# A GEGLU layer on one core: first phase over seven PSUM banks, four blocks of x transposed by TensorE

## The chip, the core and the metric

The kernel runs on one core of one Trainium2 chip. A core has five engines that run side by side and meet through semaphores: TensorE (PE; its weight loads are listed as PEld), VectorE (DVE), ScalarE (ACT), GpSimd (POOL) and SyncE (SP). Sixteen DMA engines move data between HBM and the on-chip memory SBUF. Matmul results go to PSUM, eight banks of 128 partitions by 512 fp32 values. The metric is the device time of one execution in microseconds (us), as the median of ten runs.

## The reference

```python
x: (32, 32, 1024) bf16    w_gate, w_up: (1024, 3584)    w_down: (3584, 1024)
def reference(x, w_gate, w_up, w_down):
    return (gelu_tanh(x @ w_gate) * (x @ w_up)) @ w_down
```

The leading dimensions of x make 1024 rows (tokens). 1024 is also the contraction length of the two first products: eight blocks of 128, called k here.

## The kernel before

**Tiling.** The tokens are two halves h of 512. The 3584 hidden columns are 28 chunks m of 128. One chunk and one half need a `g` product and a `u` product, each a PSUM bank that gathers eight matmuls, one for each k: 128 by 128 weights are loaded and 512 columns of x, transposed, stream past (`mm_gu`, L162). `glu` (L171) then lets ScalarE take the GELU of the `g` bank and VectorE multiply it by the `u` bank into `hT`. When all of `hT` is there, the second product runs, 28 matmuls for each of 17 output pieces, and each piece is copied and stored. Each matmul there needs the tokens' columns of `hT` as weights and `wd` as the moving operand.

**Order of work.** The program is a list that is written by hand: `pr.add` appends an operation to its engine's list with the keys that it reads and writes (`r`, `w`), and each engine runs its own list in order. Waits follow from the keys. A wait stops everything that stands behind it on the same engine, DMA issues included. The profile gives L98 for all operations, because they are all made by one line of `emit`.

**Start.** TensorE runs eight matmuls on constants (L184). x must get into `xT` with the contraction on the partitions. For half 0, blocks k=0 and 1 (`NX = 2`) are loaded plainly into `xn` by two transfers, one issued by SP and one by ACT (L191). TensorE transposes them in 128 by 128 pieces against an identity matrix, four for each block, and VectorE copies the bf16 result out of PSUM in halves of 256 columns (L205 to L212). The second half of a block has a key of its own, `("x", k, "b")`. All other blocks are transposed on the way by DMA, issued by SP (`load_x`, L195): k=2, 3, 4, 5 and 6-7 for half 0 at once, and four pairs for half 1 once a matmul of k=3 is done (L235).

Weights of the first four chunks come in pieces by k (`load_w`, L155): k=0 and 1 of `g` by SP and of `u` by ACT, 128 KB each; k=2-3 of each by ACT, 256 KB each; k=4-5 and k=6-7 of each by ACT once the last matmul of k=0, or of k=1, is done (L231). Weights of later chunks come from SP in 1 MB pieces behind that.

**First phase.** Half 0 of the chunks m=0 to 3 goes over all eight banks at once: for each k from 0 to 5, four `g` matmuls and four `u` matmuls (L221). Then, one m after another, the last two k of `g` and of `u`, and its `glu` (L223). Half 1 of the same chunks follows in a like order, starting with k=0 and 1 of each m.

Of the kernel before, what the change touches and what calls it, by code (L numbers as in the profile page):

```python
# [6 lines left out]
P = 128  # L7
BF16 = mybir.dt.bfloat16
FP32 = mybir.dt.float32
F32R = mybir.dt.float32r  # L10
ACTF = mybir.ActivationFunctionType
# [93 lines left out]
def bass_standalone__geglu_ffn__sampling_kernel(  # L105
# [11 lines left out]
    DK, TC, FM = D // P, N // P, F // P  # L117
# [3 lines left out]
    x_r = xf.rearrange("(tc p) d -> p tc d", p=P)  # L121
# [4 lines left out]
    pr = _Program()  # L126

    with ExitStack() as es:
        def sb(name, shape, dtype):
            return es.enter_context(nc.sbuf_tensor(name, shape, dtype))  # L130

        xT = sb("xT", [P, DK, N], BF16)
# [7 lines left out]
        g_b = [sb(f"g{i}", [P, 512], FP32) for i in range(NGB)]  # L140
        warm = sb("warm", [P, 2], FP32)
        ident = sb("ident", [P, P], BF16)
        xn = sb("xn", [P, 4, 2 * P], BF16)
        osb = xT
        ps = es.enter_context(nc.psum_tensor("ps", [P, 8, 512], FP32))
        const0 = nc.const_aps.tensor(0.0, [P, 1], FP32)
# [8 lines left out]
        def load_w(eng, kind, gi, k0=0, k1=DK, r=()):  # L155
            c0, n, buf, s0 = groups[gi]
            src, dst = (wg_r, wg_b) if kind == "g" else (wu_r, wu_b)
            pr.add(eng, "dma_start", dst[buf][:, k0:k1, s0 * P:(s0 + n) * P], src[:, k0:k1, c0 * P:(c0 + n) * P],
                w=[(kind, buf, s0 + i, k) for i in range(n) for k in range(k0, k1)],
                r=r, dma=f"w{kind}{gi}_{k0}")  # L160

        def mm_gu(kind, m, h, k, bank, w=()):  # L162
            buf, slot = where[m]
            wt = (wg_b if kind == "g" else wu_b)[buf]
            pr.add("pe", "matmul", ps[:, bank, :], wt[:, k, slot * P:(slot + 1) * P], xT[:, k, h * 512:(h + 1) * 512],
                start=(k == 0), stop=(k == DK - 1),
                r=[(kind, buf, slot, k), ("x", k, h)] + ([("x", k, "b")] if h == 0 else []), w=[("ps", bank), *w])

        glu_n = [0]

        def glu(m, h, bg, bu):  # L171
            g = glu_n[0] % NGB
            glu_n[0] += 1
            pr.add("act", "activation", g_b[g][:, :], ps[:, bg, :], ACTF.Gelu_apprx_tanh,
                   r=[("ps", bg)], w=[("gb", g)])
            pr.add("dve", "tensor_tensor", hT[:, m, h * 512:(h + 1) * 512], g_b[g][:, :], ps[:, bu, :], ALU.mult,
                r=[("gb", g), ("ps", bu)], w=[("h", m, h)])
# [8 lines left out]

        NX = 2
        for i, eng in enumerate(("sp", "act")):  # L190
            pr.add(eng, "dma_start", xn[:, 2 * i:2 * i + 2, :], x_r[:, 2 * i:2 * i + 2, 0:NX * P], w=[("xn", i)], dma=f"xn{i}")  # L191
        for k in range(NX):
            load_w("sp", "g", 0, k, k + 1)
            load_w("act", "u", 0, k, k + 1)
        def load_x(h, k0, k1, r=()):  # L195
            pr.add("sp", "dma_start_transpose", xT[:, k0:k1, h * 512:(h + 1) * 512],
                   xf[h * 512:(h + 1) * 512, k0 * P:k1 * P], r=r, w=[("x", k, h) for k in range(k0, k1)],
                   dma=f"x{k0}_{h}")

        for k0, k1 in ((2, 3), (3, 4), (4, 5), (5, 6), (6, 8)):  # L200
            load_x(0, k0, k1)
        load_w("act", "g", 0, 2, 4)
        load_w("act", "u", 0, 2, 4)
        pr.add("act", "activation", warm[:, 0:1], const0, ACTF.Gelu_apprx_tanh)
        for k in range(NX):  # L205
            for i, b in enumerate((6, 7) if k == 0 else (4, 5)):
                half = ps[:, b, 0:P].bitcast(BF16)
                for t in range(2):
                    pr.add("pe", "transpose", half[:, t * P:(t + 1) * P], xn[:, 2 * i + t, k * P:(k + 1) * P],
                           ident[:, :], r=[("xn", i), "ident"], w=[("ps", b)])  # L210
                pr.add("dve", "tensor_copy", xT[:, k, i * 256:(i + 1) * 256], half, r=[("ps", b)],
                       w=[("x", k, 0) if i == 0 else ("x", k, "b")])  # L212


        KO = 2
        for h in range(2):
            steps = []
            for m in range(4):
                steps += [(m, kind, k) for kind in "gu" for k in range(KO)] if h else []
            for k in range(KO if h else 0, DK - KO):  # L220
                steps += [(m, kind, k) for kind in "gu" for m in range(4)]  # L221
            for m in range(4):
                steps += [(m, kind, k) for kind in "gu" for k in range(DK - KO, DK)] + [(m, None, None)]  # L223
            for m, kind, k in steps:
                if kind is None:
                    glu(m, h, 2 * m, 2 * m + 1)
                else:
                    mm_gu(kind, m, h, k, 2 * m + (kind == "u"), w=[("mm", k)] if h == 0 and m == 3 and kind == "u" else ())
                if h == 0 and (m, kind) == (3, "u"):
                    if k < 2:  # L230
                        load_w("act", "g", 0, 2 * k + 4, 2 * k + 6, r=[("mm", k)])  # L231
                        load_w("act", "u", 0, 2 * k + 4, 2 * k + 6)
                    if k == 3:
                        for k0 in range(0, DK, 2):
                            load_x(1, k0, k0 + 2, r=[("mm", k)])  # L235
# [7 lines left out]
        u = 8  # L243
        for m in range(4, FM):
            for h in range(2):
                bg, bu = 2 * (u % 4), 2 * (u % 4) + 1
                for kind, b in (("g", bg), ("u", bu)):
                    for k in range(DK):
                        mm_gu(kind, m, h, k, b)
                glu(m, h, bg, bu)  # L250
                u += 1
            for gi in range(loaded + 1, len(groups)):
                if groups[gi][0] - 6 <= m:
                    load_w("sp", "g", gi)
                    load_w("sp", "u", gi)
                    loaded = gi
            if m >= 4 and m % 3 == 0 and wd_pieces:
                a, b_ = wd_pieces.pop(0)
                pr.add("sp", "dma_start", wd[:, a:b_, :], wd_r[:, a:b_, :],
                       r=[("h", m - 1, 1)], w=[("wd", i) for i in range(a, b_)], dma=f"wd{a}")  # L260
# [9 lines left out]
        for ji, (tc, col, n) in enumerate(jobs):  # L270
            b = ji % 8
            for m in range(FM):
                pr.add("pe", "matmul", ps[:, b, 0:n], hT[:, m, tc * P:(tc + 1) * P], wd[:, m, col:col + n],
                    start=(m == 0), stop=(m == FM - 1),
                    r=[("h", m, tc // 4), ("wd", m)], w=[("ps", b)])
            if ji % 2 == 0:
                pr.add("act", "activation", osb[:, tc, col:col + n], ps[:, b, 0:n], ACTF.Copy,
                       r=[("ps", b)], w=[("o", ji), ("x", tc, 0), ("x", tc, 1), ("x", tc, "b")])
            else:
                pr.add("dve", "tensor_copy", osb[:, tc, col:col + n], ps[:, b, 0:n],  # L280
                       r=[("ps", b)], w=[("o", ji), ("x", tc, 0), ("x", tc, 1), ("x", tc, "b")])
            pr.add("sp", "dma_start", out_r[:, tc, col:col + n], osb[:, tc, col:col + n],
                   r=[("o", ji)], dma="out")
# [34 lines left out]
```

## Time and profile before

| What | Value |
|---|---|
| Median of ten runs | 300.18 us (299.79 to 301.03) |
| The profiled execution | 300.05 us, its span 298.3 us |
| TensorE matmuls | busy 294.4 us (99%), x1388 |
| TensorE weight loads | busy 135.7 us (45%) |
| VectorE, ScalarE | busy 44.7 us (15%), 40.1 us (13%) |
| Matmuls 128x512 on wg and on wu | x448 each, mean 379 ns |
| Transposes by TensorE | x8, mean 304 ns |
| VectorE copies of 128x256 bf16 into xT | x4, mean 289 ns |
| DMA transposes | x9 issued by SP, median 5.8 us to landing |
| HBM | 22.28 MB read, 2.10 MB written |

The span is the time from the first to the last instruction that the profiler recorded; the rest of the execution's time lies around it. Busy time is summed over instructions as they are recorded, and a matmul's recorded length holds its way through the array, which overlaps with the next one. For TensorE, then, the distance from one start to the next tells the rate, and the length does not. In a timeline, rows that follow each other on one engine with the same form are merged: start, time from the first start to the last end, engine, line, operation, output and inputs, shapes and count; in brackets the idle time ahead of them and what ended it.

### The profile page before, as it was taken

Reading aid. Unit: us, or ns where it says so; the run is one execution under the profiler, and the core shown is the slowest. Engines: PE = TensorE matmul, PEld = TensorE weight load, DVE = VectorE, ACT = ScalarE, POOL = GpSimd, SP = SyncE. Lnnn points to the kernel's source line nnn. Section 1 sums busy time; section 2 is a strip of 40 time slices with the busy share of each in tenths; the row PEclk is TensorE's granted clock in tenths of the full one; section 3 lists DMA queues with packets and bytes.
Section 4 is the critical chain, followed back from the end, with each engine's and each line's share of the span. In section 5 each row is a group of like instructions: output and inputs, shape, how many; then the busy total and the mean of one; then the engine's idle time right before and its main releaser. Section 6 shows DMA issues by size and latency. Waiting matters only on the chain.

```text
span 298.3 us, 3155 instructions
## 1 busy us (share of the span) xinstructions
PE 294.4 (99%) x1388; PEld 135.7 (45%) x1388; DVE 44.7 (15%) x68; ACT 40.1 (13%) x67; POOL 0.7 (0%) x6
## 2 busy tenths in 40 slices
PE   8999999999999999999999999999999999999996
PEld 4344444444444444444444444444444444444455
DVE  1030421111221111221111122110000000000000
ACT  1030411211111121111121111110000000000000
POOL 0000000000000000000000000000000000000000
PEclk9999999999999999999999999999999999999999
DMA  7999744006608408331040030000000000010001
GB/s 163 264 244 355 230 152 119 24 0 209 215 0 288 138 11 284 128 80 62 0 143 0 0 141 2 0 0 18 20 18 34 20 18 18 18 37 18 18 18 37
DMA packets 28845, 26.42 MB, mean 89 GB/s; under 512 B 8224, under 2 KB 25248, under 8 KB 28832
## 3 DMA queue, kind: packets, MB, share of 16 engines
q1 hardware_dynamic: 26640, 24.25, 26.3%
q10 hardware_dynamic: 2192, 1.97, 2.7%
q8 instruction: 11, 0.18, 0.2%
q14 instruction: 2, 0.02, 0.0%
HBM read 22.28 MB, written 2.10 MB: 82 GB/s over the span
## 4 chain that ended last, share of the span: by engine, by line
PE 97%; DMA 2%; ACT 0%; issue 0%
PE ps L98 97%; DMA wg<-in_w_gate_dram 2%; ACT xT L98 0%
## 5 line engine op out<-in xcount | busy, mean ns | idle before, releaser
L98 PE MATMUL ps<-xT,wg 128*128 128x512 bf16 x448 | 108.1, 379 | 0.6 <-DMA wg<-in_w_gate_dram 0.5
L98 PE MATMUL ps<-xT,wu 128*128 128x512 bf16 x448 | 108.1, 379 | 0.0
L98 PE MATMUL ps<-wd,hT 128*128 128x512 bf16 (+1 forms) x476 | 96.9, 366 | 0.0
L98 PEld LDWEIGHTS ps<-wd,hT 128*128 128x128 bf16 x476 | 46.6, 98 | 50.4
L98 PEld LDWEIGHTS ps<-xT,wg 128*128 128x128 bf16 x448 | 43.6, 98 | 54.0 <-DMA wg<-in_w_gate_dram 1.5
L98 PEld LDWEIGHTS ps<-xT,wu 128*128 128x128 bf16 x448 | 43.8, 98 | 52.9 <-DMA wu<-in_w_up_dram 0.5
L98 DVE TENSOR_TENSOR hT<-g,ps 128x512 bf16<-128x512 f32 x56 | 38.5, 688 | 156.4 <-PE ps L98 156.4
L98 ACT ACTIVATE g<-ps 128x512 f32<-128x512 f32 x56 | 33.4, 597 | 159.5 <-PE ps L98 159.5
L98 DVE CAST xT<-ps 128x512 bf16<-128x512 f32 (+1 forms) x8 | 5.3, 658 | 88.1 <-PE ps L98 88.1
L98 ACT ACTIVATE xT<-ps 128x512 bf16<-128x512 f32 (+1 forms) x9 | 5.2, 573 | 93.1 <-PE ps L98 93.1
L98 PE MATMUL ps<-const-bfloat16-1.0 128*128 128x512 bf16 (+1 forms) x8 | 2.9, 545 | 0.8 <-PEq L303 0.8
L98 PEld LDWEIGHTS ps<-const-bfloat16-1.0 128*128 128x128 bf16 x8 | 1.0, 137 | 2.4 <-issue 2.4
L98 ACT ACT_TABLE_LOAD x1 | 1.3, 1283 | 3.5 <-issue 3.5
L98 DVE COPY xT<-ps 128x256 bf16<-128x256 bf16 x4 | 0.9, 289 | 4.0 <-PE ps L98 4.0
L98 PE MATMUL ps<-ident,xn 128*128 128x128 bf16 x8 | 1.0, 304 | 0.0
L98 PEld LDWEIGHTS ps<-ident,xn 128*128 128x128 bf16 x8 | 0.7, 132 | 0.2
L98 POOL TENSOR_SCALAR_AFFINE_SELECT ident<-ident 128x128 bf16<-128x128 bf16 x1 | 0.3, 292 | 0.2 <-POOL ident L98 0.2
L98 POOL MEMSET ident<- 128x128 bf16 x1 | 0.2, 204 | 0.3 <-POOLq L303 0.3
L98 ACT ACTIVATE warm<-const-float32-0.0 128x1 f32<-128x1 f32 x1 | 0.2, 203 | 0.0
L303 POOL MEMSET const-bfloat16-1.0<- 128x1 bf16 x1 | 0.1, 102 | 0.0
L303 POOL MEMSET const-uint8-127<- 128x1 uint8 x1 | 0.1, 102 | 0.0
L303 POOL MEMSET const-float32-0.0<- 128x1 f32 x1 | 0.1, 98 | 0.2 <-issue 0.2
(1 smaller groups left out, 0.1 us busy)
## 6 DMA issues: line engine op xcount, KB each, us to landing
wd<-in_w_down_dram SPq DMA_DIRECT2D x7, 1024.0 KB, 5.4
wg<-in_w_gate_dram SPq DMA_DIRECT2D x6, 1024.0 KB, 7.3
wu<-in_w_up_dram SPq DMA_DIRECT2D x6, 1024.0 KB, 9.6
out_dram<-xT SPq DMA_DIRECT2D x15, 128.0 KB, 1.7
wg<-in_w_gate_dram ACTq DMA_DIRECT2D x3, 256.0 KB, 6.3
wu<-in_w_up_dram ACTq DMA_DIRECT2D x3, 256.0 KB, 6.7
wg<-in_w_gate_dram SPq DMA_DIRECT2D x2, 128.0 KB, 3.5
wu<-in_w_up_dram ACTq DMA_DIRECT2D x2, 128.0 KB, 4.2
```

The source lines that it names most:

```text
L98: ins = getattr(eng, name)(*args, **kw)
L303: nc = _bacc.Bacc("TRN2", target_bir_lowering=False, num_devices=1)
```

## The change

The first phase of half 0 uses seven banks. Bank 7 is left to transposes, and `u` of m=3 is done in one go at the end of the half. TensorE transposes four blocks of x (`NX = 4`). Those of block 0 stand where they stood, in banks 6 and 7, with two copies of 256 columns. Those of k=1, 2 and 3 stand between the matmuls of the block before: after `g` of m=0 and 1, ahead of `g` of m=2 and 3 and `u` of m=0 to 2. They go to bank 7, and one copy of 512 columns takes each out. The columns of x for k=2 and 3 come by a plain transfer from SP, behind the first weights. The DMA transposes of half 0 shrink to k=4, 5 and 6-7, and the first of them waits for the second copy of block 0. The weights for k=2 and 3 come in four pieces of 128 KB instead of two of 256 KB, still by ACT. What was released by the last `u` matmul of m=3 (L229) is now released by that of m=2.

```diff
-                r=[(kind, buf, slot, k), ("x", k, h)] + ([("x", k, "b")] if h == 0 else []), w=[("ps", bank), *w])
+                r=[(kind, buf, slot, k), ("x", k, h)] + ([("x", k, "b")] if h == k == 0 else []), w=[("ps", bank), *w])
...
-        NX = 2
+        NX = 4
...
+        pr.add("sp", "dma_start", xn[:, :, 2 * P:NX * P], x_r[:, 0:4, 2 * P:NX * P],
+               w=[("xn", 0, 1), ("xn", 1, 1)], dma="xn2")
+        for k in range(2, 4):
+            load_w("act", "g", 0, k, k + 1)
+            load_w("act", "u", 0, k, k + 1)
...
-        for k0, k1 in ((2, 3), (3, 4), (4, 5), (5, 6), (6, 8)):
-            load_x(0, k0, k1)
-        load_w("act", "g", 0, 2, 4)
-        load_w("act", "u", 0, 2, 4)
...
+        def pe_x(k):
+            for i in range(2):
+                b = 6 + i if k == 0 else 7
+                half = ps[:, b, (0 if k == 0 else i * P):(P if k == 0 else (i + 1) * P)].bitcast(BF16)
                 for t in range(2):
                     pr.add("pe", "transpose", half[:, t * P:(t + 1) * P], xn[:, 2 * i + t, k * P:(k + 1) * P],
-                           ident[:, :], r=[("xn", i), "ident"], w=[("ps", b)])
+                           ident[:, :], r=[("xn", i, k // 2), "ident"], w=[("ps", b)])
...
+            if k:
+                pr.add("dve", "tensor_copy", xT[:, k, 0:512], ps[:, 7, 0:256].bitcast(BF16), r=[("ps", 7)],
+                       w=[("x", k, 0)])
+
+        pe_x(0)
+        for k0, k1 in ((4, 5), (5, 6), (6, 8)):
+            load_x(0, k0, k1, r=[("x", 0, "b")])
...
+            if h == 0:
+                for k in range(DK - KO):
+                    steps += [(m, "g", k) for m in range(2)] + ([("x", None, k + 1)] if k + 1 < NX else [])
+                    steps += [(m, "g", k) for m in range(2, 4)] + [(m, "u", k) for m in range(3)]
...
+                for kind in "gu":
+                    k0 = 0 if (h, m, kind) == (0, 3, "u") else DK - KO
+                    steps += [(m, kind, k) for k in range(k0, DK)]
+                steps += [(m, None, None)]
...
+                last = (h, m, kind) == (0, 2, "u")
+                mm_gu(kind, m, h, k, 2 * m + (kind == "u"), w=[("mm", k)] if last else ())
```

More of the change, by code (lines that the diff above doesn't have):

```diff
@@ L142, in bass_standalone__geglu_ffn__sampling_kernel @@
         ident = sb("ident", [P, P], BF16)
-        xn = sb("xn", [P, 4, 2 * P], BF16)
+        xn = sb("xn", [P, 4, 4 * P], BF16)
         osb = xT
@@ L185, in bass_standalone__geglu_ffn__sampling_kernel @@
             pr.add("pe", "matmul", ps[:, 3, 0:n], one[:, 0:P], one[:, 0:n], start=True, stop=True, w=[("ps", 3)])
-        NX = 2
+        NX = 4
         for i, eng in enumerate(("sp", "act")):
-            pr.add(eng, "dma_start", xn[:, 2 * i:2 * i + 2, :], x_r[:, 2 * i:2 * i + 2, 0:NX * P], w=[("xn", i)], dma=f"xn{i}")
-        for k in range(NX):
+            pr.add(eng, "dma_start", xn[:, 2 * i:2 * i + 2, 0:2 * P], x_r[:, 2 * i:2 * i + 2, 0:2 * P],
+                   w=[("xn", i, 0)], dma=f"xn{i}")
+        for k in range(2):
             load_w("sp", "g", 0, k, k + 1)
             load_w("act", "u", 0, k, k + 1)
+        pr.add("sp", "dma_start", xn[:, :, 2 * P:NX * P], x_r[:, 0:4, 2 * P:NX * P],
[3 more added lines that the diff above has]
+            load_w("act", "u", 0, k, k + 1)
+        pr.add("act", "activation", warm[:, 0:1], const0, ACTF.Gelu_apprx_tanh)
         def load_x(h, k0, k1, r=()):
@@ L198, in load_x @@
                    dma=f"x{k0}_{h}")
-        for k0, k1 in ((2, 3), (3, 4), (4, 5), (5, 6), (6, 8)):
-            load_x(0, k0, k1)
-        load_w("act", "g", 0, 2, 4)
-        load_w("act", "u", 0, 2, 4)
[L204 to L207, printed above, removed]
+        def pe_x(k):
+            for i in range(2):
+                b = 6 + i if k == 0 else 7
+                half = ps[:, b, (0 if k == 0 else i * P):(P if k == 0 else (i + 1) * P)].bitcast(BF16)
                 for t in range(2):
                     pr.add("pe", "transpose", half[:, t * P:(t + 1) * P], xn[:, 2 * i + t, k * P:(k + 1) * P],
-                           ident[:, :], r=[("xn", i), "ident"], w=[("ps", b)])
-                pr.add("dve", "tensor_copy", xT[:, k, i * 256:(i + 1) * 256], half, r=[("ps", b)],
-                       w=[("x", k, 0) if i == 0 else ("x", k, "b")])
+                           ident[:, :], r=[("xn", i, k // 2), "ident"], w=[("ps", b)])
+                if k == 0:
+                    pr.add("dve", "tensor_copy", xT[:, k, i * 256:(i + 1) * 256], half, r=[("ps", b)],
+                           w=[("x", k, "b") if i else ("x", k, 0)])
+            if k:
[4 more added lines that the diff above has]
+            load_x(0, k0, k1, r=[("x", 0, "b")])
         KO = 2
@@ L217, in bass_standalone__geglu_ffn__sampling_kernel @@
             steps = []
-            for m in range(4):
[L219 to L223, printed above, removed]
+            if h == 0:
+                for k in range(DK - KO):
+                    steps += [(m, "g", k) for m in range(2)] + ([("x", None, k + 1)] if k + 1 < NX else [])
+                    steps += [(m, "g", k) for m in range(2, 4)] + [(m, "u", k) for m in range(3)]
+            else:
+                for m in range(4):
+                    steps += [(m, kind, k) for kind in "gu" for k in range(KO)]
+                for k in range(KO, DK - KO):
+                    steps += [(m, kind, k) for kind in "gu" for m in range(4)]
+            for m in range(4):
+                for kind in "gu":
+                    k0 = 0 if (h, m, kind) == (0, 3, "u") else DK - KO
+                    steps += [(m, kind, k) for k in range(k0, DK)]
+                steps += [(m, None, None)]
             for m, kind, k in steps:
+                if m == "x":
+                    pe_x(k)
+                    continue
                 if kind is None:
                     glu(m, h, 2 * m, 2 * m + 1)
-                else:
-                    mm_gu(kind, m, h, k, 2 * m + (kind == "u"), w=[("mm", k)] if h == 0 and m == 3 and kind == "u" else ())
-                if h == 0 and (m, kind) == (3, "u"):
+                    continue
+                last = (h, m, kind) == (0, 2, "u")
+                mm_gu(kind, m, h, k, 2 * m + (kind == "u"), w=[("mm", k)] if last else ())
+                if last:
                     if k < 2:
```

## The prediction

> **What bounds the kernel now.** I read the page first (TensorE, PE, is busy 99% of the span), then the chain of waits, which says whose work ends last:
>
> ```profile
> 4.62 1.92 PE ps L98 x9
> 6.54 5.81 DMA wg<-in_w_gate_dram
> 12.35 0.05 issue
> 12.40 283.43 PE ps L98 x1340
> ```
>
> From 12.40 us to the output's last column nothing but TensorE counts, and that stretch is the same matmuls before and after. A change of the first phase can only move the point from which TensorE runs without a pause. Third, the timeline of TensorE in the first 13 us (start, length, instruction, idle time ahead and what ended it):
>
> ```profile
> 1.58 0.15 PEld L98 LDWEIGHTS ps<-const-bfloat16-1.0 128*128 128x128 bf16 x1 [0.28 <-issue]
> 2.01 0.15 PEld L98 LDWEIGHTS ps<-const-bfloat16-1.0 128*128 128x128 bf16 x1 [0.28 <-issue]
> ...
> 3.51 1.02 PE L98 MATMUL ps<-ident,xn 128*128 128x128 bf16 x8
> ...
> 4.62 1.02 PE L98 MATMUL ps<-xT,wg 128*128 128x512 bf16 x4
> 5.48 1.03 PE L98 MATMUL ps<-xT,wu 128*128 128x512 bf16 x4
> 6.34 1.03 PE L98 MATMUL ps<-xT,wg 128*128 128x512 bf16 x4
> 7.21 1.03 PE L98 MATMUL ps<-xT,wu 128*128 128x512 bf16 x4
> 8.69 1.02 PE L98 MATMUL ps<-xT,wg 128*128 128x512 bf16 x4 [0.46 <-DMA wg<-in_w_gate_dram]
> ...
> 11.28 1.03 PE L98 MATMUL ps<-xT,wu 128*128 128x512 bf16 x4
> 12.39 0.55 PEld L98 LDWEIGHTS ps<-xT,wg 128*128 128x128 bf16 x4 [0.58 <-DMA wg<-in_w_gate_dram]
> 12.40 1.04 PE L98 MATMUL ps<-xT,wg 128*128 128x512 bf16 x4
> ```
>
> Starts, not lengths, carry it: four 512-column matmuls begin every 0.863 us, 0.216 each. So the group after 7.21 was due at 8.07 and came at 8.69 (0.62 late), and the one after 11.28 was due at 12.14 and came at 12.40 (0.26 late). Both wait for weights (PE is the matmul, PEld its weight load). These **0.88 us** are all that the change can win inside the first phase. Fourth, DMA in three stretches of 1 us (8.5 to 9.5, 13.5 to 14.5, 15.5 to 16.5; q1 carries SP's transfers, q10 ACT's; packets, MB, share of all 16 engines):
>
> ```profile
> q1 hardware_dynamic: 549, 0.14, 101.5%
> ...
> q10 hardware_dynamic: 384, 0.38, 106.7%
> ...
> q1 hardware_dynamic: 1152, 0.29, 127.8%
> ```
>
> The first and last are x transposed by DMA in pieces under 512 B: 0.14 to 0.23 MB for 1 us of all engines. The middle one is plain weights: 0.36 MB. One x block of 0.131 MB thus costs 0.6 to 0.9 us as a DMA transpose and 0.36 as a plain load.
>
> **The change part by part.**
>
> *Start.* The first matmul still needs both copies of block 0. DVE makes these two from 3.96 to 4.48 (0.52), and the first weight load comes at 4.59; TensorE has begun its last transpose at 4.26. The four transposes of block 1 that leave this place were in the shadow of the second copy: gain 0, bounds -0.1 (a quicker wake-up) to 0.
>
> *Transposes in the stream.* Three groups of four now stand among the matmuls. In the old start eight take from 3.51 to a last start of 4.26, one interval of them lengthened by a landing; 0.107 each is left. But TensorE runs at half speed there (the granted clock of the profile's slices, 9 throughout, does not show it): the warm-up loads at 1.58 and 2.01 stand 0.43 apart for 512 columns, twice the 0.216 of later. So a transpose at full speed lies between 0.054 (half) and 0.107. I take 0.065, near the lower row, since 256-column matmuls at the end take about 0.11, exactly half of 512. 12 x 0.065 = **+0.78** (0.65 to 1.28). They can't be hidden, for TensorE is the bound.
>
> *Copies.* Behind each group stand five matmuls (1.08 us) before block k+1 is needed. Old rows: 0.04 from the end of a transpose of 0.30 to the copy, and 0.14 from the copy's end to the next matmul. A 512-column copy is put at 0.29 + 0.23 = 0.52 (the second of two adds 0.23); the 128x512 CAST, 0.66, is the upper end. 0.30 + 0.04 + 0.52 + 0.14 = 1.00, under 1.08: cost 0, with the upper end 3 x 0.06 = 0.2.
>
> *Reordering.* u of m=3 goes to the end in bank 7: 64 matmuls as before, 0. Its last GLU still ends the half, and the first h=1 matmuls use banks freed earlier than before.
>
> *Queues.* SP now waits for the second copy (about 4.5) with three DMA transposes behind it, 1.25 us each to issue (the timeline has them at 2.21, 3.46, 4.76), and behind those the four for h=1, which wait for a matmul at about 11.8 anyway. So blocks 4, 5 and 6-7 are issued at 4.55, 5.8 and 7.1; before, at 4.76, 6.06 and 7.37. Earlier, then, though the first two blocks' issues are gone. ACT issues four pieces of 128 KB where it had two of 256 KB: at 0.46 to 0.73 each done by 4.5, its table load of 1.28 after that by 5.8, before its next job.
>
> *The weight waits.* With 0.26 per group, blocks begin at 4.62, 6.39, 8.16, 9.93, 11.44, 12.95, and k=6 at 14.46. The plain load of x blocks 2 and 3 is needed at 6.82. Ahead of it in both rings stand, with its own, 1.31 MB; 0.08 MB have come by 2.5, then 0.35 MB per us as from 2.5 to 3.5: it lands at 6.0, spare 0.8. Weights of k=2 come with it, needed 8.16. Weights of k=4,5 are asked for at 6.58 (now 6.54) and needed from 11.44 (now due 12.14, landing 12.35). From 6.0 the rings owe k=3's and these weights, 0.79 MB (2.2 us), and at most four transposed blocks (2.3 to 3.7): 10.5 to 11.9. Only if all transposes pass first is this late; I take 0 waits left, so **-0.88**, bounds -0.88 to -0.3. Weights of k=6,7 add 0.52 MB (1.5 us): 12.0 to 13.4, needed 14.5 to 14.9 (they landed at 14.57 and 15.44).
>
> [...]
>
> *Clock.* In the old start TensorE pauses 0.26 us (4.36 to 4.62) and is at full speed from 4.62 on. Now the pause is 0.68 (from 3.94). If full speed comes later, each 512-column matmul costs 0.21 more; a whole first block, 7 x 0.21 + 4 x 0.05 = 1.7. And what was hidden by the waits of 0.88 for executions that get to full speed late no longer is: I put **+0.2** for that, between 0 and 0.88. The ten runs spread over 1.24 us (299.79 to 301.03), so something like it varies.
>
> [...]
>
> *Sum* against the profiled execution's own time: 300.05 (span 298.3, 1.75 around it) + 0 + 0.78 - 0.88 + 0.2 = 300.15. That execution lies 0.13 under the median of 300.18, so as a median **300.3**.
>
> **The rivals.**
> 1. *The low clock stays* (slower). Place: the pause before the first matmul, 0.26 to 0.68; price 1.7 for one block at half speed, up to 3 for two: 301.2 to 303. It decides once half speed lasts over three matmuls of the first block (3 x 0.21 = 0.6). For it: TensorE is at half speed up to the last transpose at 4.26, hardly ahead of the first matmul. Against it: 3.2 us of work without a pause still precede (0.77 to 3.94). 0.16.
> 2. *The waits move, and the change doesn't free DMA.* The transposes for blocks 4 to 7 now run exactly while the weights for k=4 to 7 come; k=6,7 are needed 1.3 us earlier, because a block has 7 matmuls. For it: TensorE's 0.26 at 12.40 already came from that mix. Price: u of k=6 at its old 15.44 would be 0.55 late: 300.3 + 0.55, range 300.6 to 301.2. Against: two blocks fewer are transposed (1.2 to 1.9 us of all engines), and the 0.7 us of plain load in their place comes before the mix. 0.15.
> 3. *Faster.* Transposes at 0.054, all waits gone, no late clock, and the wake-up 0.1 sooner: 300.05 + 0.65 - 0.88 - 0.1 = 299.7; with the old median's waits larger than this execution's, 299.3 to 299.6. 0.07.
>
> **How the numbers follow.** Forecast (waits gone, transposes about as dear, 299.7 to 300.8): 0.62. About 0.2% (0.6 us) is what a measurement of this kernel can tell from no change, so within means 299.58 to 300.78: nearly all of the forecast and 0.03 of rival 2, together 0.63. Slower: rival 1, the rest of rival 2 and the forecast's edge, 0.30. Faster: 0.07. The range goes from 299.7 (rival 3's upper edge, below it 0.08) to 301.3, into rival 1 (above it 0.12).
>
> **What would show it.** Twelve transposes as three groups with about 0.26 us from the last matmul before to the first after; over 0.4 refutes the price. No idle time of TensorE put down to DMA between 4.6 and 16 us; any is rival 2. Starts of the first g matmuls 0.216 apart; 0.43 is rival 1. A wait for DVE in front of k=1, 2 or 3 means that the copy is late. The uninterrupted stretch should begin at 4.6. If the first matmul moves from 4.62 by over 0.1 us, the first step is wrong.

## The result, and the profile after

The changed kernel takes 301.04 us (median of 16 runs, 300.61 to 301.55). The kernel before, with the runs beside it, stands at 300.05 (57 runs, 299.13 to 301.25). The ratio is 1.0034 with a 95% interval of [1.0024, 1.0044]: **slower by 0.34%**, about 1 us. That lies within the range given (299.7 to 301.3), but above the 300.8 at which the forecast itself ended, and beyond the 0.2% within which the likeliest case had put it.

The profiled execution took 301.28 us with a span of 299.5, against 300.05 and 298.3 before. Its chain of waits (start, length, what; "issue" is time in which the engine waited for nothing that the profile shows):

```profile
2.17 0.04 issue
2.21 6.00 DMA xn<-in_x_dram
8.21 0.05 issue
8.26 288.84 PE ps L98 x1371
```

Before, the chain went from a load of weights that landed at 12.35 into TensorE's unbroken stretch. Now it goes from the plain load of x blocks 2 and 3 (the x load, from here on), landing at 8.21. TensorE never waits again after that. The weights that ended last before no longer appear. The timeline of TensorE up to there:

```profile
4.77 1.01 PE L98 MATMUL ps<-xT,wg 128*128 128x512 bf16 x2 [0.48 <-DVE xT L98]
5.58 0.63 PE L98 MATMUL ps<-ident,xn 128*128 128x128 bf16 x4
6.01 0.70 PE L98 MATMUL ps<-xT,wg 128*128 128x512 bf16 x2
6.54 0.81 PE L98 MATMUL ps<-xT,wu 128*128 128x512 bf16 x3
7.19 0.59 PE L98 MATMUL ps<-xT,wg 128*128 128x512 bf16 x2
8.26 0.40 PE L98 MATMUL ps<-ident,xn 128*128 128x128 bf16 x4 [0.47 <-DMA xn<-in_x_dram]
8.49 0.59 PE L98 MATMUL ps<-xT,wg 128*128 128x512 bf16 x2
```

Three things are read from the starts. (a) From 4.77 to 6.54 stand four 512-column matmuls and four transposes. At full speed that is 4 x 0.216 + 4 x 0.056 = 1.09 us; it took 1.77. So TensorE ran at half speed until about 6.2 (the first two of these matmuls take from 4.77 to 5.58, 0.40 each, against the 0.216 of later ones) and lost **0.68**. (b) The two matmuls from 7.19 were done at 7.62, and the transposes of block 2 came at 8.26: a wait of **0.64**. (c) Four transposes at full speed take 8.49 - 8.26 = 0.23, thus 0.057 each.

The account against the profile before, by the start of the output's last matmul (1.27 us later): first matmul 4.77 instead of 4.62, +0.15; half speed +0.68; twelve transposes 12 x 0.056 = +0.67; the new wait +0.64; the two old waits -0.88. Sum +1.26, for 1.23 measured between the two executions. This is a sum along TensorE's rows and does not say what would be gained if one term went: with full speed from 4.77 TensorE would have been ready for block 2 at 6.94, and the wait would have been 1.32 instead of 0.64.

### The profile page after: what moved, and what is told of

Same layout as the page of the kernel before. It is cut to its first block, busy times and chain, and to the rows that moved or that the text cites. A ratio compares the mean times of both kernels' runs of the same rounds, so it can differ in the third digit from the quotient of the medians.

```text
span 299.5 us, 3174 instructions
## 1 busy us (share of the span) xinstructions
PE 295.4 (99%) x1396; PEld 136.4 (46%) x1396; DVE 45.6 (15%) x69; ACT 40.1 (13%) x67; POOL 0.7 (0%) x6
## 4 chain that ended last, share of the span: by engine, by line
PE 96%; DMA 2%; SPq 0%; ACT 0%; issue 0%
PE ps L98 96%; DMA xn<-in_x_dram 2%; SPq L98 0%; ACT xT L98 0%
## 5 line engine op out<-in xcount | busy, mean ns | idle before, releaser
L98 DVE COPY xT<-ps 128x512 bf16<-128x512 bf16 (+1 forms) x5 | 1.8, 371 | 9.1 <-PE ps L98 9.1
L98 PE MATMUL ps<-ident,xn 128*128 128x128 bf16 x16 | 2.0, 263 | 0.5 <-DMA xn<-in_x_dram 0.5
L98 PEld LDWEIGHTS ps<-ident,xn 128*128 128x128 bf16 x16 | 1.3, 113 | 2.1 <-DMA xn<-in_x_dram 1.2
```

Of the source, the lines that this page charges most:

```text
L98: ins = getattr(eng, name)(*args, **kw)
```

## The experiments

All kernels are edits of the changed one, except the pieces alone, which edits the kernel before. Ratios are to the kernel before. Times of one profile and of its own execution belong together. Half speed and DMA varied between the profiled executions: with the x load issued alike, 0.68, 0.90 and 0 us were lost to half speed, and it landed at 8.21, 8.24 and 8.52 (the changed kernel, block 1 in the pause, the DMA transposes held back). The runs of the changed kernel spread over 0.94 us, those of the kernel before over 2.12. So a profile is one sample, and the verdicts go by the medians.

My theory after the traces: the wait for the x load sets the end, and half speed costs only where no transfer ends last. The rival: the pause of TensorE ahead of the first matmul, through the clock, is the whole loss.

### TensorE's pause filled with constants

```diff
         pe_x(0)
+        for _ in range(4):
+            pr.add("pe", "matmul", ps[:, 3, 0:P], one[:, 0:P], one[:, 0:P], start=True, stop=True, w=[("ps", 3)])
```

> The changed kernel with four 128-column matmuls on constants put behind the four transposes of block 0, so that TensorE's pause ahead of the first real matmul shrinks from some 0.7 us to 0.3. Clock theory (the pause delays full speed): the starts of the first g matmuls are 0.216 apart instead of 0.38 to 0.43, 0.5 to 0.7 us are saved, median about 300.4, ratio to the kernel before 1.001 to 1.002. Rival (when full speed comes is chance and the pause has no part in it; only the transfer of x blocks 2 and 3 counts): median stays at 301.0, ratio 1.003 to 1.004, and the wait for that transfer stays at 0.6 us or grows.

Measured: 300.75 (300.45 to 300.96, 8 runs), ratio 1.0018 [1.0003, 1.0034]. In its profile the first matmuls were still at half speed (0.49 us lost), the load landed at 7.5 and the wait was 0.14. Between the two theories, and its interval overlaps that of the changed kernel: it decides nothing alone.

### TensorE's pause filled with the transposes of block 1

```diff
-                b = 6 + i if k == 0 else 7
+                b = (6 + i, 5, 7, 7)[k]
...
-                pr.add("dve", "tensor_copy", xT[:, k, 0:512], ps[:, 7, 0:256].bitcast(BF16), r=[("ps", 7)],
+                pr.add("dve", "tensor_copy", xT[:, k, 0:512], ps[:, b, 0:256].bitcast(BF16), r=[("ps", b)],
...
         pe_x(0)
+        pe_x(1)
...
-                    steps += [(m, "g", k) for m in range(2)] + ([("x", None, k + 1)] if k + 1 < NX else [])
+                    steps += [(m, "g", k) for m in range(2)] + ([("x", None, k + 1)] if 1 < k + 1 < NX else [])
```

> The changed kernel with the transposes of block 1 put back to the start (bank 5), so that eight transposes stand in the stream instead of twelve... of them only eight, and the pause is filled with useful work. Clock theory: full speed before the first matmul as in the kernel before, 0.7 us saved, and 4 x 0.056 = 0.2 us more for the transposes that leave the stream; but what is saved ahead of block 2 can turn into a longer wait for the transfer of x blocks 2 and 3, which sets when block 2 begins (8.26 us). With that transfer as the end, the gain is near 0 and TensorE's wait for it grows from 0.6 to 1.5 us. Rival that chance alone sets the clock: first g matmuls as often 0.43 as 0.216 apart, and again no gain.

Measured: 301.25 (300.69 to 301.55, 6 runs), ratio 1.0035 [1.0022, 1.0048]. Four transposes less in the stream and no pause, and nothing gained. In its profile 0.90 us was lost to half speed, with the pause filled. The chain of waits of its profile says why:

```profile
2.21 6.03 DMA xn<-in_x_dram
8.29 4.07 PE ps L98 x24
```

The load lands at 8.24, and from there TensorE's work ends last. Time saved ahead of that landing turned into wait: TensorE was ready for block 2 at 7.54, 0.08 sooner than in the changed kernel's profile, and waited 0.75 instead of 0.64.

### The DMA transposes held back

```diff
-        for k0, k1 in ((4, 5), (5, 6), (6, 8)):
-            load_x(0, k0, k1, r=[("x", 0, "b")])
...
                     pe_x(k)
+                    if k == 1:
+                        for k0, k1 in ((4, 5), (5, 6), (6, 8)):
+                            load_x(0, k0, k1, r=[("x", 1, 0)])
```

> The changed kernel with the DMA transposes of half 0 held back until block 1 is copied (about 6.7 us) instead of block 0 (4.5 us). Theory that these transposes hold up the end of the load of x blocks 2 and 3 (its last 512 B packets begin by 7.6 us, its landing is told at 8.21): it lands by 7.6, the wait of 0.64 us is gone, and the low DMA rate between 4.6 and 5.4 us (124 GB/s) is gone if the issue of a transpose causes it; ratio about 1.0015. Rival (the load is late by its own): landing at 8.0 to 8.2 again, low rate stays, ratio 1.0034 or more, because blocks 4 and 5 now land 2 us later, still before their use at 11.7.

Measured: 301.08 (300.96 to 301.78, 5 runs), ratio 1.0041 [1.0027, 1.0055]. The theory that the queued transposes hold up the x load falls: nothing is gained. Its profile also separates the two terms, since here TensorE happened to be at full speed from the first matmul:

```profile
4.72 0.59 PE L98 MATMUL ps<-xT,wg 128*128 128x512 bf16 x2 [0.47 <-DVE xT L98]
5.16 0.38 PE L98 MATMUL ps<-ident,xn 128*128 128x128 bf16 x4
5.38 0.59 PE L98 MATMUL ps<-xT,wg 128*128 128x512 bf16 x2
5.81 0.81 PE L98 MATMUL ps<-xT,wu 128*128 128x512 bf16 x3
6.46 0.59 PE L98 MATMUL ps<-xT,wg 128*128 128x512 bf16 x2
8.56 0.40 PE L98 MATMUL ps<-ident,xn 128*128 128x128 bf16 x4 [1.51 <-DMA xn<-in_x_dram]
```

From 4.72 to 5.81 is 1.09, so no half speed at all; but the load landed at 2.20 + 6.32 = 8.52, the wait was 8.56 - 6.89 = 1.67, and the execution took 301.58. Set beside the other two: landing 8.21 and 301.28, 8.24 and 301.32, 8.52 and 301.58. The difference is 293.07, 293.08 and 293.06, with 0.68, 0.90 and 0 us lost to half speed. The fill with constants, whose load landed at about 7.5 for 300.60, fits as well. In these profiles, where this load ends last, the time is its landing plus 293.07 within 0.02, and neither the clock nor the transposes ahead of it count. That speaks against the rival that the clock is the whole loss: this execution lost nothing to half speed and at 301.58 was slower than the changed kernel's 301.28.

### The x load split over two rings

A ring is the DMA queue of one issuing engine: q1 for SP's transfers, q10 for ACT's.

```diff
-        pr.add("sp", "dma_start", xn[:, :, 2 * P:NX * P], x_r[:, 0:4, 2 * P:NX * P],
-               w=[("xn", 0, 1), ("xn", 1, 1)], dma="xn2")
+        for i, eng in enumerate(("sp", "act")):
+            pr.add(eng, "dma_start", xn[:, 2 * i:2 * i + 2, 2 * P:NX * P], x_r[:, 2 * i:2 * i + 2, 2 * P:NX * P],
+                   w=[("xn", i, 1)], dma=f"xm{i}")
```

> The changed kernel with the plain load of x blocks 2 and 3 split over SP's and ACT's rings, 128 KB each, so that less stands ahead of each half. Transfer theory (the 256 KB on SP's ring end too late, landing at 8.21): both halves land by 7.6, the wait of 0.64 us goes, ratio falls by 0.002 to about 1.0015. Rival (all DMA engines are slow from 4.6 to 5.5 us whatever the ring, or the DMA transposes behind hold up the landing): landing stays at 8.0 or later and the time at 301.0.

Measured: 300.45 (299.79 to 301.89, 12 runs), ratio 1.0020 [1.0007, 1.0032]. The transfer theory holds: the halves land at 6.7 and 7.0, no wait is left, and the median is 0.6 us under the changed kernel's. What appears instead is a spread of 2.1 us, and the profiled execution was the slowest, 301.89:

```profile
4.83 1.01 PE L98 MATMUL ps<-xT,wg 128*128 128x512 bf16 x2 [0.48 <-DVE xT L98]
5.64 0.63 PE L98 MATMUL ps<-ident,xn 128*128 128x128 bf16 x4
6.07 1.06 PE L98 MATMUL ps<-xT,wg 128*128 128x512 bf16 x2
6.92 1.48 PE L98 MATMUL ps<-xT,wu 128*128 128x512 bf16 x3
8.20 0.84 PE L98 MATMUL ps<-xT,wg 128*128 128x512 bf16 x2
8.88 0.39 PE L98 MATMUL ps<-ident,xn 128*128 128x128 bf16 x4
```

Nine matmuls and four transposes from 4.83 to 8.88: 2.17 us at full speed, 4.05 here. The five matmuls from 6.07 to 8.20 take 0.43 each. Half speed cost 1.88, and with no transfer at the end all of it is in the time. In two later profiles of versions with the split the halves landed only at about 7.2 to 7.6, just as TensorE, at half speed before, was ready for them: the margin is small.

### The x load ahead of the weights of k=1

```diff
         for k in range(2):
-            load_w("sp", "g", 0, k, k + 1)
-            load_w("act", "u", 0, k, k + 1)
+            if k == 0:
+                load_w("sp", "g", 0, k, k + 1)
+            load_w("act", "u" if k == 0 else "g", 0, k, k + 1)
+        load_w("act", "u", 0, 1, 2)
```

> The load of x blocks 2 and 3 put ahead of the g weights of k=1 on SP's ring; these weights go to ACT's ring. Theory that the load is late because of what stands ahead of it on its ring: 128 KB less there, at 0.15 to 0.18 MB per us and ring, is 0.7 to 0.9 us: landing at 7.3 to 7.5, wait gone, median about 300.4 as with the split. Rival (the landing depends on the sum of both rings alone): landing at 8 or later; or the g weights of k=1, now third on ACT's ring, come late for block 1 and take the wait over.

Measured: 300.68 (300.11 to 302.27, 12 runs), ratio 1.0022 [1.0009, 1.0036]. Like the split, the load lands early, at about 6.8, the wait is gone, and half speed shows: in the profiled execution (302.27) it lasted to the transposes at 9.15 and cost 2.14. The landing is earlier than the 7.3 to 7.5 expected, and the median gains less. Two other things help the landing here: the load is issued 0.47 sooner, at 1.74, and between 4.5 and 5.5 us the DMA engines moved 0.33 MB, where the changed kernel's profile has 0.14. So it fits that what stands ahead on the ring made the load late, but one profile does not separate the three.

### The table load moved

```diff
-        pr.add("act", "activation", warm[:, 0:1], const0, ACTF.Gelu_apprx_tanh)
...
                         load_w("act", "u", 0, 2 * k + 4, 2 * k + 6)
+                    if k == 0:
+                        pr.add("act", "activation", warm[:, 0:1], const0, ACTF.Gelu_apprx_tanh)
```

> The changed kernel with ScalarE's table load (1.28 us from 4.22 in its trace) moved behind the weight loads of k=4 and 5. In the four profiles so far in which block 2 waits for its x, the execution's time is the landing of that load plus 293.07 us, within 0.02, so the median tells the landing. Theory that the table load makes the low DMA rate from 4.5 to 5.5 us: the rate stays at 0.3 MB per us or above there, the load lands about 0.6 us sooner, at 7.6, ratio about 1.0015. Rival (the low rate has another cause): 0.15 to 0.2 MB per us again, median 301.0.

Measured: 301.04 (300.98 to 301.17, 5 runs), ratio 1.0034 [1.0022, 1.0046]: no change in the median, as the rival said. In the one profile 0.25 MB moved between 4.5 and 5.5 us, between the two expectations, and as much as in two profiles with the table load in its old place (the split, and block 1 in the pause, 0.25 each). There the x load landed at 7.4, and another transfer ended last, the u weights of k=4 and 5:

```profile
7.53 5.79 DMA wu<-in_w_up_dram
13.32 0.05 issue
13.36 283.43 PE ps L98 x1340
```

So the median does not tell the landing here, and the cause of the low rate stays open. The weight waits of the kernel before are not gone for good: they can come back when the x load lands early.

### Split, and block 1 at the start

The diff of the split, and of the edit above that fills the pause with block 1, together; in short:

```diff
-        pr.add("sp", "dma_start", xn[:, :, 2 * P:NX * P], x_r[:, 0:4, 2 * P:NX * P],
-               w=[("xn", 0, 1), ("xn", 1, 1)], dma="xn2")
+        for i, eng in enumerate(("sp", "act")):
+            pr.add(eng, "dma_start", xn[:, 2 * i:2 * i + 2, 2 * P:NX * P], x_r[:, 2 * i:2 * i + 2, 2 * P:NX * P],
+                   w=[("xn", i, 1)], dma=f"xm{i}")
...
         pe_x(0)
+        pe_x(1)
```

> The load of x blocks 2 and 3 split over both rings (it then landed at 6.96) together with block 1 transposed at the start. Once the transfer no longer ends last, TensorE's own work does: four transposes fewer in the stream, 4 x 0.056 = 0.22 us less than the split alone (300.45), median 300.2, ratio about 1.001, with runs between 299.6 and 301.5 according to when full speed comes. If the split alone was still held by a transfer: no gain over it, 300.45.

Measured: 300.38 (299.55 to 300.61, 11 runs), ratio 1.0010 [0.9999, 1.0021]. Lower than the split alone by 0.07 in the median and by 0.24 in the fastest run; the expected 0.22 is not resolved: the medians hardly differ, and the fastest runs are one execution each. Its chain of waits has TensorE alone from 4.72 on:

```profile
4.72 291.48 PE ps L98 x1380
```

### Split, and the pause filled with constants

The same split, with this in place of the transposes of block 1:

```diff
         pe_x(0)
+        for _ in range(4):
+            pr.add("pe", "matmul", ps[:, 3, 0:P], one[:, 0:P], one[:, 0:P], start=True, stop=True, w=[("ps", 3)])
```

> The split load of x blocks 2 and 3, with four matmuls on constants in TensorE's pause ahead of the first real matmul. The split alone is bound by TensorE and spreads from 299.79 to 301.89; its profile shows half speed until 8.85 us. [...] Rival (chance alone): spread of 2 us and median 300.45 as with the split.

Measured: 300.22 (299.65 to 300.64, 11 runs), ratio 1.0006 [0.9996, 1.0016]. The rival's spread of 2 us and median of 300.45 did not come: the spread is 0.99 instead of 2.1, the slowest run 1.25 lower than the split's, the median 0.23 lower. That is the direction of the clock theory, by which the pause delays full speed. It is not shown by that: the medians' intervals overlap, and the spread of the split rests on the 3 of its 12 runs that lie above 301. In its profile TensorE still lost 0.8 us at half speed (4.61 to 6.51 is 1.90 instead of 1.09) and was at full speed from there.

```profile
3.92 0.63 PE L98 MATMUL ps<-const-bfloat16-1.0 128*128 128x128 bf16 x4
4.61 1.01 PE L98 MATMUL ps<-xT,wg 128*128 128x512 bf16 x2
5.41 0.64 PE L98 MATMUL ps<-ident,xn 128*128 128x128 bf16 x4
5.84 0.84 PE L98 MATMUL ps<-xT,wg 128*128 128x512 bf16 x2
6.51 0.81 PE L98 MATMUL ps<-xT,wu 128*128 128x512 bf16 x3
```

This does not differ from the kernel before by more than the measurement tells; no version tried beats it.

### Blocks 2 and 3 by DMA transpose again

```diff
-        NX = 4
+        NX = 2
...
-        pr.add("sp", "dma_start", xn[:, :, 2 * P:NX * P], x_r[:, 0:4, 2 * P:NX * P],
-               w=[("xn", 0, 1), ("xn", 1, 1)], dma="xn2")
...
+        for k0, k1 in ((2, 3), (3, 4), (4, 5), (5, 6), (6, 8)):
+            load_x(0, k0, k1)
         pe_x(0)
-        for k0, k1 in ((4, 5), (5, 6), (6, 8)):
-            load_x(0, k0, k1, r=[("x", 0, "b")])
```

> Seven banks and the transposes of block 1 in the stream kept, but x blocks 2 and 3 by DMA transpose again and at once, as in the kernel before. If the weights of k=4 and 5 are again what ends last (12.35 in the kernel before), then with seven banks 4 matmuls fewer have been done by then, 0.86 us more are left behind it: median 300.9, ratio 1.003, wait of 1 us or more at block 4. Rival (the plain load of blocks 2 and 3 is the whole loss): the loss goes, median 300.0 to 300.2.

Measured: 300.52 (299.53 to 301.29, 11 runs), ratio 1.0013 [1.0001, 1.0026]. Between the two. My wait of 1 us is not in the profile: that execution (299.57, the second fastest of the eleven) had full speed from the first matmul and no wait at all. Neither statement holds as put; the next run takes it apart.

### Seven banks without transposes in the stream

```diff
-                b = 6 + i if k == 0 else 7
+                b = 6 + i if k == 0 else 5
...
         pe_x(0)
+        pe_x(1)
...
-                    steps += [(m, "g", k) for m in range(2)] + ([("x", None, k + 1)] if k + 1 < NX else [])
+                    steps += [(m, "g", k) for m in range(2)]
```

This edits the version with blocks 2 and 3 by DMA transpose; the copy of block 1 reads bank 5.

> Seven banks in the first phase and the weights in 128 KB pieces, but both blocks 0 and 1 transposed at the start and blocks 2 to 7 by DMA, as before: no transpose in the stream. Against the version with the four transposes of block 1 in the stream (300.52) TensorE has 4 x 0.056 = 0.22 us less to do and no pause before the first matmul: 300.0 to 300.3, ratio 1.000 to 1.001. If the seven banks by themselves cost (each block has 0.22 us less work to cover its transfers): waits of 0.3 to 0.9 us at blocks 2 to 4 and ratio 1.001 to 1.003.

Measured: 300.85 (299.69 to 302.26, 12 runs), ratio 1.0027 [1.0011, 1.0044]. With nothing of the transposes in the stream it is slower than the kernel before, and its profile has the waits of the second statement: the groups that begin at 8.61, 10.36 and 11.96 are 0.22, 0.25 and 0.09 late, and the u matmuls of k=4 wait until 13.45, 0.62 late (one of the three has no record):

```profile
11.96 1.04 PE L98 MATMUL ps<-xT,wg 128*128 128x512 bf16 x4
13.45 0.82 PE L98 MATMUL ps<-xT,wu 128*128 128x512 bf16 x2 [0.46 <-DMA wu<-in_w_up_dram]
```

Seven banks leave each block 7 x 0.216 = 1.51 us of work to cover its transfers instead of 1.73. That this is why the waits come is argued: the kernel before with the smaller pieces, the next run, has one of 1.15 with eight banks.

### The smaller weight pieces alone, in the kernel before

```diff
-        load_w("act", "g", 0, 2, 4)
-        load_w("act", "u", 0, 2, 4)
+        for k in range(2, 4):
+            load_w("act", "g", 0, k, k + 1)
+            load_w("act", "u", 0, k, k + 1)
```

> The kernel before with one part of the change alone: the weights of k=2 and 3 come in four pieces of 128 KB in order of use instead of two of 256 KB. Theory that its wait at block 2 (0.62 us) was the size of these pieces: that wait shrinks, but x block 2 by DMA transpose landed at 8.55, hardly before the weights' 8.60, so at most some 0.2 us go there and the wait at block 4 takes up the rest: ratio 0.999 to 1.000. Rival, from the version with blocks 2 and 3 by DMA transpose, whose profile shows no wait at all: both waits go, ratio 0.997 to 0.998.

Measured: 300.14 (299.34 to 301.13, 12 runs), ratio 1.0007 [0.9995, 1.0020]: nothing. In its profile the wait at block 2 is gone, and the u weights of k=4 and 5 take it over:

```profile
12.04 1.03 PE L98 MATMUL ps<-xT,wg 128*128 128x512 bf16 x3
14.05 1.04 PE L98 MATMUL ps<-xT,wu 128*128 128x512 bf16 x4 [0.98 <-DMA wu<-in_w_up_dram]
```

One of the four matmuls of the first group has no record; the second group was due at 12.90. In this profile 0.53 us was also lost to half speed (the first eight matmuls take from 4.61 to 6.86), with the start of the kernel before.

## Why the prediction was right or wrong

*Right.* The bound and the place: all of the difference lies ahead of TensorE's unbroken stretch. The price of a transpose at full speed: 0.057 against the 0.065 taken, 0.67 against 0.78 for twelve. The copies: 0.42 long, under the 0.52 taken, and no group waits for one. The start: the first matmul came at 4.77 for 4.62, more than the 0.1 that the prediction had named as a sign that this step is wrong, but the transposes ahead of it began 0.17 later as well, with the x halves; in other versions with the same start the first matmul came between 4.61 and 4.93. The two old waits: 0.88 gone from the profile.

*The number* lies in the range, but by the range's width and not by the forecast's path: that path had no wait left and ended at 300.8, and what covers 301.04 is rival 2's stretch of it, 300.6 to 301.2, whose transfer was another one (below). The signs named for both of them appeared, first g matmuls about 0.40 apart (rival 1) and idle time put down to DMA between 4.6 and 16 us (rival 2).

*The step that failed* is the weight waits, in the sentence that the plain load of x blocks 2 and 3 "lands at 6.0, spare 0.8". It landed at 8.21 and was needed at 7.62 (6.94 at full speed). I had taken 0.35 MB per us from one good microsecond and carried it to the end. Two stretches of the profile after, DMA from 4.5 to 5.5 us and from 6 to 7, show two errors (queue, packets, MB, share of all 16 engines):

```profile
q1 hardware_dynamic: 87, 0.06, 34.9%
q10 hardware_dynamic: 98, 0.09, 33.9%
```

```profile
q10 hardware_dynamic: 249, 0.23, 65.3%
q1 hardware_dynamic: 278, 0.14, 45.9%
```

In the first stretch both rings together moved 0.14 MB, not 0.35, which alone is 0.6 us. In the second the rate is back at 0.37, but SP's ring gets 0.14 of it: about as many packets as ACT's, of 512 B instead of 1 KB. The sum had given each ring half of the bytes, with ACT's ring stopped at what block 2 needs; it goes on with later weights. The split moves half of the load to the other ring, and in its profile the same work lands by 7.0.

Two more things could be read. The low rate stood in the profile before, in the same stretch from 4.5 to 5.5 us, 0.15 MB:

```profile
q10 hardware_dynamic: 93, 0.09, 59.4%
q1 hardware_dynamic: 242, 0.07, 36.5%
```

And the sum let the load land with its last byte: in the profile after, from 7.6 on SP's ring begins only pieces under 512 B, those of the transposes (288 packets and 0.07 MB up to 8.2), and the landing is told at 8.21, 0.6 us later. The profile before has such a gap too: the 256 packets of SP's first x load had begun by 2.9, and it landed at 3.4.

*The clock.* The +0.2 was under what the profile has, 0.68, but in the changed kernel it costs nothing while the x load ends last. It counts once the load is early: the split alone shows 1.88 us of half speed in one execution. So rival 1 named a price that exists (301.89 and 302.27 lie in its 301.2 to 303) and a place where, in the kernel as changed, a transfer covered it; that the pause is its cause is not shown (below). Rival 2 had the right form, a wait that moves, and the wrong transfer: the g and u weights of k=6 and 7 came at 13.5 and 14.2, and no one waited.

*What the 0.34% is made of,* by the medians: the split takes it to 0.20%, with the pause filled as well to 0.06%; the last two intervals, [1.0024, 1.0044] for the change and [0.9996, 1.0016] with both, are apart, the single steps overlap. The sum of the result section (first matmul, half speed, transposes in the stream, new waits, old waits) also holds for the other eleven profiled executions, each to 0.06 us: for the split 301.93 against 301.89, for the split with the pause filled 300.64 against 300.64. In this last one 0.67 us of transposes and 0.81 of half speed stand against 0.88 of vanished waits. That the medians are made up in the same way fits, but is not measured. Shown is that the x load ends the chain in the profiles of the change, of the version with block 1 in the pause and of the one with the DMA transposes held back, whatever half speed took there, and that with the load split its wait is gone and the median 0.6 us lower.

*Open.* What lowers the DMA rate between 4.5 and 5.5 us: with the table load moved it was 0.25 MB, with the DMA transposes held back 0.22. Why the fill without the split came out at 1.0018 while the transposes of block 1 in the same pause gave 1.0035: the intervals overlap, but five of the six executions of the second lie above all eight of the first. In the profiles the x load landed at 7.5 in the first and at 8.24 in the second, and nothing here says why.

## What to carry to other kernels

Follow a moved transfer to its own due time with the rate that its own ring gets (here 0.14 of the 0.37 MB that moved from 6 to 7 us), and not with the best rate of all rings (0.35 MB per us in the prediction); waits that are removed at 8 and 12 us are given back if a new load is due at 7.6 and lands at 8.2. Work that was taken off ahead of the transfer that ends last bought nothing here (301.25 with block 1's transposes in the pause, against 301.04), so look at the chain's last landing first: time minus landing was constant to 0.02 us. And half speed in TensorE's first microseconds cost nothing while a transfer covered it, and up to 2.1 us in one execution when none did; filling the pause ahead of the first matmul may help, which is not settled here.

## What the runs showed of the hardware that I had not expected

- The point at which TensorE reached full speed (512-column matmuls 0.216 us apart instead of 0.40 to 0.43) varied, between executions of versions with the same start, from the first matmul (4.72) to about 8.7 and 9.3 us. Over all thirteen profiled executions the loss to half speed was 0 in three, 0.49 to 0.90 in eight, where most of the points lie between 5.7 and 6.5 us, and 1.88 and 2.14 in two. These two are among the six with a pause of about 0.7 us ahead of the first matmul, as are two of those without any loss; the seven others lost 0.90 at most. That the pause makes the late ones is a guess from two executions. The spreads fit it only in part: 2.1 and 2.2 us for the split and for the x load ahead with the pause, 1.0 and 1.1 for the two split versions without, but 2.1 for the kernel before and 2.6 for the seven banks alone, which have no such pause and wait for weights.
- Two rings side by side got about the same number of packets between 6 and 7 us, 278, nearly all of 512 B, and 249 of 1 KB, in the profile after: the ring with the smaller packets got 0.14 MB against 0.23. It is not a rule of these runs: with the table load moved, the two got 271 and 108 packets between 4.5 and 5.5 us.
